# Scores of the mLSTM chunks as four 64x64 products, without their masked quarter

## The chip, the cores and the metric

The kernel runs on one core of a Trainium2 chip. The metric is the device time of one execution in microseconds (us). A comparison uses the median of several executions; the profile is one execution taken by the hardware profiler.

## The reference

The program joins two blocks. The first is an mLSTM cell over batch 4, 8 heads, 768 tokens and head size 40; the second is a feed-forward block on the 3072 tokens with 320 features, 2048 hidden units and exact GELU.

```python
for t in range(S):
    m_new = np.maximum(f_gate[:, :, t] + m, i_gate[:, :, t])
    f_stab = np.exp(f_gate[:, :, t] + m - m_new)
    i_stab = np.exp(i_gate[:, :, t] - m_new)
    m = m_new
    C = f_stab[..., None, None] * C + i_stab[..., None, None] * np.einsum('bhd,bhe->bhde', vt, kt)
    n = f_stab[..., None] * n + i_stab[..., None] * kt
    h_tilde = np.einsum('bhde,bhe->bhd', C, qt)
    denom = np.maximum(np.abs(np.einsum('bhd,bhd->bh', n, qt)[..., None]), 1.0)
    y[:, :, t] = sigmoid(o_gate[:, :, t]) * h_tilde / denom
x = y.transpose(0, 2, 1, 3).reshape(B * S, H * D)
h = x @ w_in
out = (0.5 * h * (1.0 + erf(h / sqrt(2)))) @ w_out
```

## The kernel before, in words

The 768 tokens are cut into 6 chunks of 128 (index `c`, 0 to 5). A cell is one chunk of one batch, `n = 4 * c + b`. Inside a chunk the recurrence is written as attention: `scores` computes k·q for the 128 source tokens s (partitions) and the 128 target tokens t (columns) of each of the 8 heads. The result is multiplied by decay weights W, and `values` multiplies the product with v. What came before the chunk enters through a carried state (`carry`, and `carry_two` for two batches at once from chunk 2 on). Weights are zero where s > t, so a quarter of each head's 128x128 scores (s in the second half, t in the first) is computed and then multiplied by zero.

Heads go in pairs. In the transposed tiles kT and qT one head of a pair lies on partitions 0 to 63 and the other on 64 to 127 (`halves`, index `hip`); the 40 features of a head are padded to 64. For each pair `scores` (L469) issues two products of 64 rows, 128 stationary and 128 moving columns (L479), one in each half of the array's rows, into two PSUM banks. VectorE then multiplies each bank by the weights with one 128x512 instruction (L482).

The other operations that the prediction follows, by line:

- `load` (L129, issue at L135): q, k, v and o-gate of a cell into SBUF, one transfer each, issued by SP. From chunk 2 on q and k for the scores come by `load_blocks` (L138, issues at L145) and are transposed by VectorE (`turn_half`, L430). The token-major k and v are still loaded for the state and the values; three buffers take turns. `load_M` (L154, L162 and L165) brings the running maximum, from which W is made.
- `mask` (L378, L381): GpSimd's affine_select writes 1e30 where s > t. `weights` (L384, L407): ScalarE turns the tile into exp(-M + a), head by head, with the per-token bias aT on partitions.
- `weigh_values` (L464, L466): v times ewT, again a factor for each partition. It feeds the products of v and k that update the state (L538 in `carry_two`); L531 there is the product of q with the old state. VectorE takes L531's result (L547) and updates the state (L554 on GpSimd, L555 on VectorE).
- `values` (L564): L573 on TensorE, L581 on VectorE. `finish` (L583, L586 to L591), `twice` (L597), `turn_y` (L599, L608 and L618) and `split_x` (L623) normalise y and turn it into the input of the feed-forward block.
- `up` (L747, L768 and L779 on TensorE, L783 on ScalarE) and `down_steps` (L831, L844 on TensorE; L857, L861, L867, L874 on the others) are the feed-forward block of a chunk. L682 are sums of the second weight matrix, made once while chunk 1's products run; L672 and L700 to L702 are sums needed by its products.
- `gates_turned` (L215, L222): the gate tables aT, ewT and gT are transposed by TensorE and copied by VectorE, once at the start.

The order is written out by hand: `FRONT` for the first two chunks and the conversion of the 64-bit weights, and `DOWN` for each later chunk, in which the letters of chunk c + 1's cell steps stand between the products F of chunk c's feed-forward block. In `DOWN` M is mask, W weights, S scores, C carry_two, V values, K and Q the transposes of k and q, D weigh_last, Y finish, X turn_y, R split_x, L and B the loads for the last batch, Z and N sums on VectorE:

```python
M0 Z M1 W0 F L3 F B3 W1 Z Z F S0 Z S1 K2 C0 M2 Z G0 G1 G2 G3 V0 Z V1 W2 Z F Q2 K3 Q3 Y0 M3 D3 F F W3 F Z S2 S3
C2 V2 V3 F N F Y1 X0 R0 Y2 F F Y3 X1 R1 F X2 R2 F X3 R3 F
```

So the attention of a chunk has two rounds: S0 S1 C0 V0 V1, and S2 S3 C2 V2 V3. Each engine keeps to the order of its own instructions.

Of the kernel before, what the change touches and what calls it, by code (L numbers as in the profile page):

```python
# [14 lines left out]
OP = mybir.AluOpType  # L15

P = 128
# [22 lines left out]
def kernel(  # L40
# [16 lines left out]
    nc = tc.nc  # L57

    B, H, S, D = q.shape
    L = P  # L60
    NCH = S // L
    NP = H // 2
# [7 lines left out]
    R = P // 2  # L70
# [30 lines left out]
    aT = const.tile([P, NCH, BH], F32, name="aT")  # L101
    ewT = const.tile([P, NCH - 1, BH], F32, name="ewT")
    gT = const.tile([P, NCH - 1, BH], F32, name="gT")
# [22 lines left out]
    def out_of(n):  # L126
        return ob[n % NLD].rearrange("p (h d) -> p h d", d=D)

    def load(n, first=0, end=4):  # L129

        if n >= NCH * B:
            return
        c, b = divmod(n, B)
        for src, dst in ((q, qb), (k, kb), (v, vb), (o_gate, None))[first:end]:
            nc.sync.dma_start(out=dst[turn_of(n)][:, :, 0:D] if dst else out_of(n),  # L135
                              in_=src[b, :, c * L:(c + 1) * L, :].rearrange("h p d -> p h d"))

# [12 lines left out]
    def turn_of(n):  # L150

        return n % NLD if n < 2 * B else (n - 2 * B) % NQ
# [19 lines left out]
    for t in vb:  # L172
# [4 lines left out]
                            pattern=[[0, P]], channel_multiplier=1)  # L177
    nc.gpsimd.memset(beyond, 0.0)
    nc.gpsimd.affine_select(out=beyond, in_=beyond, compare_op=OP.is_ge, fill=1.0e30, base=0, pattern=[[1, L]],
                            channel_multiplier=-1)  # L180
# [7 lines left out]
    a = gates.tile([BH, NCH, L], F32, name="a")  # L188
    M = gates.tile([BH, NCH, L], F32, name="M")
    ew = gates.tile([BH, NCH - 1, L], F32, name="ew")  # L190
    gg = gates.tile([BH, NCH - 1, L], F32, name="gg")
# [4 lines left out]
    for j in range(3):  # L196
        m = slice(BH * j, BH * (j + 1))
# [16 lines left out]

    def gates_turned(*parts):  # L215

        for src, dst in parts:
            n = dst.shape[1]
            pg = ps_tr.tile([P, n, BH], F32, name="pg", tag="tr")
            for c in range(n):  # L220
                nc.tensor.transpose(pg[:, c, :], src[:, c, :], ident[0:BH, 0:BH])
            nc.vector.tensor_copy(out=dst, in_=pg)  # L222

    def gates_of(c0, c1):

        flat = lambda t: t[:, c0:c1].rearrange("p c l -> p (c l)")
        nc.vector.tensor_tensor_scan(out=flat(bl), data0=flat(keep), data1=flat(f_sb), initial=0.0,
                                     op0=OP.mult, op1=OP.add)
        nc.vector.tensor_tensor(out=a[:, c0:c1], in0=i_sb[:, c0:c1], in1=bl[:, c0:c1], op=OP.subtract)
        for c in range(c0, c1):  # L230
            nc.vector.tensor_tensor_scan(out=M[:, c], data0=a[:, c], data1=a[:, c], initial=m0[:, c:c + 1],
                                         op0=OP.max, op1=OP.max)
            if c + 1 < NCH:
                nc.vector.tensor_tensor(out=m0[:, c + 1:c + 2], in0=bl[:, c, L - 1:L], in1=M[:, c, L - 1:L],
                                        op=OP.add)

    def decays_of(e0, e1, g0, g1):

        e, g = slice(e0, e1), slice(g0, g1)
        nc.vector.tensor_tensor(out=ew[:, e], in0=a[:, e], in1=M[:, e, L - 1:L].to_broadcast([BH, e1 - e0, L]),  # L240
                                op=OP.subtract)
        nc.vector.tensor_tensor(out=gg[:, g], in0=m0[:, g0 + 1:g1 + 1].unsqueeze(2).to_broadcast([BH, g1 - g0, L]),
                                in1=M[:, g0 + 1:g1 + 1], op=OP.subtract)
        nc.scalar.activation(out=ew[:, e], in_=ew[:, e], func=AF.Exp)
        nc.scalar.activation(out=gg[:, g], in_=gg[:, g], func=AF.Exp)

    def decays_turned(e0, e1, g0, g1):
        e, g = slice(e0, e1), slice(g0, g1)
        gates_turned((ew[:, e], ewT[:, e]), (gg[:, g], gT[:, g]))

    def decays_last(g0, g1):
        g = slice(g0, g1)
        pd = ps_tr.tile([P, g1 - g0, BH], F32, name="pd", tag="tr")
        nc.tensor.matmul(pd.rearrange("p c n -> p (c n)"), last, gT[:, g].rearrange("p c n -> p (c n)"),
                         start=True, stop=True)
        nc.vector.tensor_copy(out=dec[:, g], in_=pd)
# [4 lines left out]
    for j in range(3):  # L261
        part = M_parts[BH * j:BH * (j + 1)]
        nc.vector.tensor_copy(out=part, in_=left)
        if j < 2:
            nc.vector.tensor_tensor(out=M_left[:, j], in0=left, in1=part, op=OP.subtract)
            left = M_left[:, j]
    gates_turned((a[:, 0:1], aT[:, 0:1]))
    warm(6)

    def second_gates():  # L270
        gates_of(1, 2)
        nc.sync.dma_start(out=M_d[0], in_=M[:, 1])
        gates_turned((a[:, 1:2], aT[:, 1:2]))
        decays_of(0, 2, 0, 1)

    def later_gates():
        gates_of(2, NCH)
        nc.sync.dma_start(out=M_d[1:].rearrange("c p l -> p c l"), in_=M[:, 2:])
        gates_turned((a[:, 2:], aT[:, 2:]))
        decays_of(2, NCH - 1, 1, NCH - 1)  # L280


# [1 line left out]
    for name, w in (("in", moe_w_in), ("out", moe_w_out)):  # L284
        rows, cols = w.shape
# [66 lines left out]
    halves = (slice(0, R), slice(R, P))  # L352
# [7 lines left out]
    def unread(bank):  # L360
        for _ in range(idle[0]):
            nc.tensor.matmul(bank, ident, ident, start=True, stop=True, skip_group_check=True)
        idle[0] = 0
# [4 lines left out]
    class Cell:  # L368
# [9 lines left out]
        def mask(self, b):  # L378

            t = Mb[self.c * B + b]  # L380
            nc.gpsimd.affine_select(out=t, in_=t, compare_op=OP.is_ge, fill=1.0e30, base=0,  # L381
                                    pattern=[[0, H], [1, L]], channel_multiplier=-1)

        def weights(self, b):  # L384

# [83 lines left out]
        def scores(self, b):  # L469
            n = self.c * B + b  # L470
            kT, qT = self.kT.pop(b), self.qT[b]

            pool, tag = (ps_tr, "tr") if self.c > 0 and b % 2 else (ps_mm, "a")
            ps = [pool.tile([P, NP, L], F32, name="ps", tag=tag) for hip in range(2)]
            unread(ps[0][:, 0, :])
            for p in range(NP):
                for hip in range(2):
                    r = halves[hip]
                    nc.tensor.matmul(ps[hip][:, p, :], kT[r, p, :], qT[r, p, :], start=True, stop=True)  # L479
            for hip in range(2):  # L480
                w = W[n].rearrange("p (m two) t -> p m two t", two=2)[:, :, hip, :]
                nc.vector.tensor_tensor(out=w, in0=ps[hip], in1=w, op=OP.mult)  # L482

        def carry(self, b):

# [72 lines left out]
        def read(self, b):  # L558

            self.reads.append(b)  # L560
            if self.c > 1 and self.reads.count(b) == 2:
                load(self.c * B + b + NQ, 1, 3)
# [36 lines left out]
        def turn_y(self, b):  # L599
            n, t = self.c * B + b, slice(b * L, (b + 1) * L)  # L600
            if self.c > 0:
                px = ps_tr.tile([P, NX + 1, L], F32, name="px", tag="tr")
            else:
                px = ps_mm.tile([P, NX + 1, L], F32, name="px", tag="b")
            unread(px[:, 0, :])
            for k in range(NX + 1):
                y = ob[n % NLD][:, k * P:(k + 1) * P] if k < NX else y_rest.rearrange("p two r -> p (two r)")
                nc.tensor.transpose(px[:, k, :], y, ident)  # L608
            self.turned.append(b)
            if len(self.finished) > len(self.turned):  # L610
                self.twice(b + 1)
            if self.c == 0:
                nc.scalar.copy(out=first_x[:, :, t], in_=px)
                return
            self.px[b] = px
            if "x" not in parts:
                parts["x"] = raw.tile([P, NX + 1, TG], F32R, name="x_hi", tag="x", bufs=1)
            nc.scalar.activation(out=parts["x"][:, :, t], in_=px, func=AF.Copy, scale=PART)  # L618
            if self.c == 1 and b < NQ:
                load(n + NLD, 1, 3)  # L620
            load(n + NLD, 3, 4)
# [18 lines left out]
    w_sums, parts, fars, w_hi, w_lo, w_mid = [], {}, [], [], [], {}  # L640
# [268 lines left out]
    def cell_steps(c, letters, before=None):  # L909
# [7 lines left out]
    first_g = Hidden(False)  # L917
    n_pieces = range(len(pieces))
    steps = dict(P=fetch, L=lambda n: load(n, 0, 2), O=lambda n: load(n, 2, 4), B=load_M, E=second_gates, N=later_gates,
                 I=keep_clock, k=warm, D=lambda: decays_turned(0, 2, 0, 1), Q=lambda: decays_turned(2, NCH - 1, 1, NCH - 1),  # L920
                 d=lambda: decays_last(0, 1), q=lambda: decays_last(1, NCH - 1),
                 A=in_turn(first_up_steps(0)), U=in_turn(first_up_steps(1)), F=in_turn(first_down_steps(first_g)),
# [4 lines left out]
    for c in range(1, NCH):  # L927
        g, later, steps = Hidden(True), [], {}
# [5 lines left out]
        products, late = down_steps(c, g)  # L934
# [32 lines left out]
```

## Time and profile before

| | us |
|---|---|
| median of 3 runs | 484.65 (484.27 to 485.49) |
| the profiled execution's own time | 484.47 |
| its span, first to last instruction | 482.7 |
| TensorE busy, of the span | 473.8 |
| VectorE | 346.4 |
| ScalarE | 222.3 |
| GpSimd | 69.5 |
| L479, the scores' products: records, mean of one | 384, 279 ns |
| L482, the multiplication by weights: instructions, mean of one | 48, 682 to 685 ns |
| L381, masks: instructions, mean of one | 20, 1.09 to 1.14 us |

In the lines of the profile, PE is TensorE's products, PEld its weight loads, DVE VectorE, ACT ScalarE, POOL GpSimd, and SPq the queue of SP, which issues transfers. L and a number is a line of the kernel. A float32 product appears as two records. Products overlap in the array, so the duration of one record is longer than the distance to the next; the distance is what counts in a row of them. The granted TensorE clock is 1.000 over the whole span.

### The profile page before, as it was taken

The numbers are of one execution on the slowest core, as the hardware profiler recorded it, in microseconds if no ns is written. First come the engines' busy times: TensorE is split into PE (matmuls) and PEld (weight loads), VectorE is DVE, ScalarE is ACT, GpSimd is POOL, SyncE is SP. The second block draws the span as 40 slices with busy tenths as digits, with TensorE's granted clock in tenths as the row PEclk, the third lists the DMA queues.
The fourth block names the chain that finished last, engine by engine and source line by source line (L and its number), as shares of the span: only waits on it lengthen the run. The fifth ranks groups of instructions, "written<-read, shape, count | busy, mean of one in ns | idle before, by whom it ended". The sixth has DMA issues, their size and how long they took to land.

```text
span 482.7 us, 11369 instructions
## 1 busy us (share of the span) xinstructions
PE 473.8 (98%) x4484; PEld 413.6 (86%) x4484; DVE 346.4 (72%) x744; ACT 222.3 (46%) x477; POOL 69.5 (14%) x108
## 2 busy tenths in 40 slices
PE   7999999999999999999999999999999999999997
PEld 7788888877777999977999977999977899977997
DVE  7899699898979997747498757498857397724321
ACT  6977999844632941112951113961103852112300
POOL 3001200001000234200144200145000212000000
PEclk9999999999999999999999999999999999999999
DMA  9998955379320365921264922265921250100001
GB/s 174 202 220 180 208 145 140 90 184 218 104 27 7 36 126 76 206 50 22 31 117 72 216 50 25 29 127 75 205 49 22 32 90 3 47 9 0 1 1 54
DMA packets 168021, 44.28 MB, mean 92 GB/s; under 512 B 154176, under 2 KB 161504, under 8 KB 167968
## 3 DMA queue, kind: packets, MB, share of 16 engines
q1 hardware_dynamic: 167968, 43.56, 46.4%
q8 instruction: 35, 0.57, 0.5%
q14 instruction: 18, 0.15, 0.1%
HBM read 39.52 MB, written 4.01 MB: 90 GB/s over the span
## 4 chain that ended last, share of the span: by engine, by line
PE 91%; DVE 4%; SPq 1%; ACT 1%; DMA 1%; issue 1%; DVEq 0%
PE po L844 32%; PE pu L768 21%; PE po L821 7%; PE pu L713 6%; PE pu L779 6%; PE ph L573 5%; PE ps L479 5%; PE pf L531 2%; PE pu L719 2%; PE px L608 2%; PE pf L538 1%; SPq L135 1%; PE pt L453 1%; ACT g L783 1%; PE pf L498 1%; DMA ob<-in_o_gate_dram 1%
## 5 line engine op out<-in xcount | busy, mean ns | idle before, releaser
L844 PE MATMUL po<-w_out,g 128*128 128x160 f32 x640 | 91.2, 300 | 0.0
L844 PEld LDWEIGHTS po<-w_out,g 128*128 128x128 f32 x640 | 87.8, 190 | 1.8 <-ACT g L783 1.8
L783 ACT ACTIVATE g<-pu 128x512 f32<-128x512 f32 x80 | 40.8, 616 | 53.5 <-PE pu L779 53.3
L844 PE MATMUL po<-w_sums,sums 128*128 128x160 f32 x320 | 47.2, 302 | 0.0
L844 PEld LDWEIGHTS po<-w_sums,sums 128*128 128x128 f32 x320 | 44.2, 190 | 0.4
L618 ACT ACTIVATE x_hi<-px 128x384 fp32r<-128x384 f32 x20 | 9.8, 489 | 70.6 <-PE px L608 70.6
L768 PE MATMUL pu<-x_hi,w_in_hi 128*128 128x512 f32 x160 | 41.7, 402 | 0.0
L700 DVE TENSOR_TENSOR sums<-g 128x512 f32<-128x512 f32 x20 | 13.8, 689 | 38.6 <-ACT g L783 38.6
L768 PE MATMUL pu<-x_lo,w_in_lo 128*128 128x512 f32 x160 | 40.7, 396 | 0.0
L407 ACT ACTIVATE W<-W,aT 128x128 f32<-128x128 f32 x128 | 39.1, 389 | 0.4 <-POOL W L381 0.2
L482 DVE TENSOR_TENSOR W<-ps,W 128x512 f32<-128x512 f32 x40 | 25.5, 685 | 15.9 <-ACT W L407 10.9
L768 PEld LDWEIGHTS pu<-x_hi,w_in_hi 128*128 128x128 f32 x160 | 28.5, 188 | 9.4 <-ACT g L783 4.1
L768 PEld LDWEIGHTS pu<-x_lo,w_in_lo 128*128 128x128 f32 x160 | 30.1, 188 | 7.2
L821 PE MATMUL po<-w_out,g 128*128 128x320 f32 x128 | 35.3, 434 | 0.0
L857 DVE TENSOR_TENSOR o_sb<-po,o_sb 128x320 f32<-128x320 f32 (+1 forms) x27 | 12.6, 465 | 28.9 <-PE po L844 24.8
L821 PEld LDWEIGHTS po<-w_out,g 128*128 128x128 f32 x128 | 24.0, 190 | 9.8 <-DVE w_out L348 0.2
L768 PE MATMUL pu<-x_all,w_in_mid 128*128 128x512 f32 x80 | 31.7, 396 | 0.1
L783 ACT ACT_TABLE_LOAD x5 | 6.4, 1283 | 55.1 <-DMA blocks<-in_k_dram 27.5
L768 PE MATMUL pu<-x_all,w_mid 128*128 128x512 f32 x80 | 31.7, 396 | 0.0
L419 POOL MEMSET g<- 32x1024 f32 x8 | 7.6, 944 | 155.8 <-ACT W L407 155.6
L713 PE MATMUL pu<-first_x,w_in 128*128 128x256 f32 x128 | 28.9, 382 | 0.0
L381 POOL TENSOR_SCALAR_AFFINE_SELECT W<-W 128x1024 f32<-128x1024 f32 x16 | 18.1, 1137 | 67.3 <-DMA W<-M_d 58.9
(180 smaller groups left out, 907.8 us busy)
## 6 DMA issues: line engine op xcount, KB each, us to landing
W<-M_d SPq DMA_DIRECT2D x16, 512.0 KB, 5.7
bits<-in_moe_w_in_dram SPq DMA_DIRECT2D x20, 256.0 KB, 4.1
bits<-in_moe_w_out_dram SPq DMA_DIRECT2D x16, 320.0 KB, 3.6
ob<-in_o_gate_dram SPq DMA_DIRECT2D x24, 160.0 KB, 3.9
out_dram<-o_sb SPq DMA_DIRECT2D x24, 160.0 KB, 1.9
vb<-in_v_dram SPq DMA_DIRECT2D x22, 160.0 KB, 5.1
kb<-in_k_dram SPq DMA_DIRECT2D x22, 160.0 KB, 4.8
g<-M_d SPq DMA_DIRECT2D x4, 512.0 KB, 4.2
```

What stands on the lines that cost most here:

```text
L381: nc.gpsimd.affine_select(out=t, in_=t, compare_op=OP.is_ge, fill=1.0e30, base=0, pattern=[[0, H], [1, L]], channel_multiplier=-1)
L407: nc.scalar.activation(out=W[n][:, h, :], in_=src, func=AF.Exp, scale=-1.0, bias=aT[:, self.c, r:r + 1])
L479: nc.tensor.matmul(ps[hip][:, p, :], kT[r, p, :], qT[r, p, :], start=True, stop=True)
L482: nc.vector.tensor_tensor(out=w, in0=ps[hip], in1=w, op=OP.mult)
L573: nc.tensor.matmul(ph[r, h, :], Pm[:, h, r], vb[turn_of(n)][:, h, :], start=True, stop=True)
L700: nc.vector.tensor_tensor(out=s1, in0=a21, in1=a22, op=OP.add)
L713: nc.tensor.matmul(banks[-1][e][:, i - i0, :], in_tile(i, x)[:, e, i % 2 * P:(i % 2 + 1) * P], first_x[:, x, t0:t1], start=(x == 0 and i = ...
L768: nc.tensor.matmul(pus[i][e], w[k][:, e, i * P:(i + 1) * P], x[:, k, :], start=(n == 0 and k == 0), stop=False, skip_group_check=True)
L779: nc.tensor.matmul(pu[e], w[r, i // 2, i % 2 * P:(i % 2 + 1) * P], x[r, NX, :], start=False, stop=(n == 2), skip_group_check=True)
L783: nc.scalar.activation(out=g.t[:, HF * e + i, :], in_=pu[e], func=AF.Gelu, scale=4097.0)
L821: nc.tensor.matmul(po[b], g.t[:, f, b * L:(b + 1) * L], w_out[:, f, :], start=(f == 0), stop=(f == NF - 1))
L844: nc.tensor.matmul(bank[at][:, i, :], lhs(j, t), rhs(j), start=(first and i == 0 and j == 0), stop=(i == n - 1 and j == HF - 1), skip_grou ...
```

## The change

For chunks 2 to 5 a head's scores are computed in products of 64 source tokens: the first 64 source tokens against all 128 targets, the second 64 against the last 64 targets only. The masked quarter is never computed. Four of these stand side by side in the array: two by rows (the heads of a pair), and two by columns (a pair of heads 0 to 3, and a pair of heads 4 to 7). For that, heads 4 to 7 keep the two halves of the source tokens swapped on the partitions: the first 64 tokens lie on partitions 64 to 127. What has source tokens on partitions follows: token-major k and v are loaded in three transfers instead of one, the mask has three parts, and the gate tables aT and ewT get two more copies each for these heads. The multiplication by weights covers only what was computed, in three regions for each bank. Values and state sum over all source tokens, so they stay as they are.

```diff
         for src, dst in ((q, qb), (k, kb), (v, vb), (o_gate, None))[first:end]:
+            if dst and n >= 2 * B:
+                x, to = src[b, :, c * L:(c + 1) * L, :].rearrange("h p d -> p h d"), dst[turn_of(n)][:, :, 0:D]
+                h0, h1 = slice(0, H // 2), slice(H // 2, H)
+                nc.sync.dma_start(out=to[:, h0], in_=x[:, h0])
+                for i in range(2):
+                    nc.sync.dma_start(out=to[halves[i], h1], in_=x[halves[1 - i], h1])
+                continue
...
             nc.vector.tensor_copy(out=dst, in_=pg)
+            if rotated:
+                there, here = [t.rearrange("p c (b h) -> p c b h", h=H)[:, :, :, H // 2:] for t in (dst, pg)]
+                for i in range(2):
+                    nc.vector.tensor_copy(out=there[R * i:R * i + R], in_=here[R * (1 - i):R * (1 - i) + R])
...
-            nc.gpsimd.affine_select(out=t, in_=t, compare_op=OP.is_ge, fill=1.0e30, base=0,
-                                    pattern=[[0, H], [1, L]], channel_multiplier=-1)
+            if self.c < 2:
+                parts = ((t, 0),)
+            else:
+                parts = ((t[:, 0:H // 2], 0), (t[0:R, H // 2:], -R), (t[R:P, H // 2:, 0:R], 0))
+            for x, base in parts:
+                nc.gpsimd.affine_select(out=x, in_=x, compare_op=OP.is_ge, fill=1.0e30, base=base,
+                                        pattern=[[0, x.shape[1]], [1, x.shape[2]]], channel_multiplier=-1)
...
-            for p in range(NP):
-                for hip in range(2):
-                    r = halves[hip]
-                    nc.tensor.matmul(ps[hip][:, p, :], kT[r, p, :], qT[r, p, :], start=True, stop=True)
+            if self.c < 2:
+                products = [(slice(0, P), p, slice(0, P), slice(0, P)) for p in range(NP)]
+            else:
+                products = [(halves[x ^ y], y * NP // 2 + p, halves[x], slice(R * x, P))
+                            for p in range(NP // 2) for x in range(2) for y in range(2)]
+            for rows, p, s_half, t in products:
+                for r, bank in zip(halves, ps):
+                    nc.tensor.matmul(bank[rows, p, t], kT[r, p, s_half], qT[r, p, t], start=True, stop=True)
+            every, m = slice(0, P), NP // 2
+            regions = (((every, slice(0, NP), every),) if self.c < 2 else
+                       ((every, slice(0, NP), halves[1]), (halves[0], slice(0, m), halves[0]), (halves[1], slice(m, NP), halves[0])))
             for hip in range(2):
                 w = W[n].rearrange("p (m two) t -> p m two t", two=2)[:, :, hip, :]
-                nc.vector.tensor_tensor(out=w, in0=ps[hip], in1=w, op=OP.mult)
+                for x in regions:
+                    nc.vector.tensor_tensor(out=w[x], in0=ps[hip][x], in1=w[x], op=OP.mult)
```

## The prediction

> **What bounds the kernel now.** I read the busy shares first, then the chain of waits in order of time, then the stretches of one stage, then the order of VectorE's instructions. The page says that TensorE is nearly always occupied:
>
> ```profile
> PE 473.8 (98%) x4484; PEld 413.6 (86%) x4484; DVE 346.4 (72%) x744; ACT 222.3 (46%) x477; POOL 69.5 (14%) x108
> ```
>
> The chain of waits (start, length, what) shows what that means from 157 us on: one TensorE block follows the other with hardly a gap. This is the attention part of chunk 3 (counting from 0), and that of the last chunk:
>
> ```profile
> 238.66 1.99 PE ps L479 x32
> 240.64 1.07 PE pf L531 x64
> 241.71 1.06 PE pf L538 x32
> 242.78 1.87 PE ph L573 x64
> 244.64 8.89 PE po L844 x64
> ...
> 384.50 1.99 PE ps L479 x32
> 386.49 1.07 PE pf L531 x64
> 387.56 2.00 PE ph L573 x64
> ```
>
> The scores of two batches (L479), then carry (L531, L538), then values (L573). Values need the scores multiplied by the decay weights on VectorE (L482). So VectorE has the carry's 2.1 us as cover in most chunks, and 1.1 us in the last chunk, which has no L538. Each chunk does this twice (batches 0 and 1, then 2 and 3).
>
> How loaded is VectorE there? In the stretch between the two rounds (length, then PE, PEld, DVE, ACT, POOL busy) it works 8.35 of 8.90 us:
>
> ```profile
> 244.60:253.50 8.90, 8.90 (x68) 8.73 (x66) 8.35 (x18) 3.73 (x13) 2.66 (x4) 1.00 0.74 149
> ```
>
> The chunk with 311 us shows its order in the timeline (start, length from first start to last end):
>
> ```profile
> 312.77 2.48 DVE L482 TENSOR_TENSOR W<-ps,W 128x512 f32<-128x512 f32 x4 [2.84 <-ACT W L407]
> 315.17 1.41 DVE L430 STREAM_TRANSPOSE kT<-blocks 64x512 f32<-64x512 f32 x2
> 316.62 0.57 DVE L547 TENSOR_TENSOR far<-pf,gT 128x164 f32<-128x164 f32 x2
> 317.10 0.65 DVE L555 TENSOR_TENSOR state<-state,pf 64x164 f32<-64x164 f32 x2
> ```
>
> The transposes follow the multiplications without a gap, so what makes L482 longer makes everything up to the next round later. The 2.84 before L482 is idle time; the label names ScalarE, but L482 starts 1.29 us after the scores start, when they end.
>
> **What the Trainium skill says.** "TensorEngine Tiling (Array Packing)", Tiling Modes: tiles of 64x64 work independently, four at once, and changing the mode drains the array. The trace agrees: L531, already 64x64, needs 1.07/16 = 67 ns for four records; and inside a score block the pairs follow every 112 ns, so 16 pairs make 1.79 of the 1.99 us, the other 0.20 being the block's two edges. "TensorE: Matmul & The Clock Gate", LDWEIGHTS: a load costs columns/1.2, 53 ns for 64 columns whatever the rows; L573, with 41 moving columns, needs 1.87/32 = 58 ns for two, so loads bound it. "VectorE: DVE Perf Modes", Two Vector instructions with no wait between them: an instruction that starts in another group of partitions than the one before waits until that has ended. The trace agrees: two L547 of 320 ns on all partitions take 0.57 together, two L555 of 317 ns on the lower and then the upper half 0.65. A handoff on the same quadrant is thus 0.083 us early, one across halves 0.013 late.
>
> **The change, part by part.**
>
> *TensorE.* Per cell, 8 products of 64 rows x 128 columns (16 records, in twos) become 16 of 64x64 (32 records, in fours): two fours of 128 moving columns and two of 64, two records each. One record of 128 columns paces at 112 ns (above); 64 columns take half, and not less than the weight load: 58 ns. A cell: 4 x (112 + 58) = 0.68 us instead of 0.90. Two cells: 1.36 + 0.10 for entry = 1.46, as the next block (L531) has the same tile shape and no edge. Saved: 1.985 - 1.46 = **0.525 us per round**, 8 rounds (4 chunks x 2): 4.2 us if nothing else moved. That fours keep their pace at 128 columns is not shown: L538 moves different data through two column tiles at 58 ns for two records of 34 ns streaming each, less than one after the other. Bound the other way: serial column tiles, 212 + 112, make a round 0.7 us longer than now.
>
> *VectorE.* Each 128x512 multiplication (682 ns) becomes three: 128x256, lower 64x128, upper 64x128. From 512 and 164 elements, time is elements/0.96 + 0.15 us: 0.416, 0.283, 0.283 (the skill's VectorE page, TRN2 errata, prices the same operation at (N+151)/0.96, an estimate within 10 ns). One bank: 0.416 - 0.083 + 0.283 + 0.013 + 0.283 = 0.912, where it was about 0.60. A round: 4 x 0.912 + 3 x 0.013 = 3.69 instead of 2.48, **+1.20 us**. It starts 0.18 earlier, so it ends 1.02 later.
>
> *First round.* Times from its start. VectorE: starts 1.11; the second batch's fifth piece ends at 1.11 + 1.85 + 1.54 = 4.50, so its second head may go at 4.57. TensorE: 1.46 + 1.05 (L531) + 0.95 (L538) + 0.94 (first values) + 0.12 (first head) = 4.52. Stall 0.05: the round gains 0.5 in the chunks at 238 and 311. At 164 two weight sums (0.47 us, L682) lie between the batches' multiplications: stall 0.52, gain 0. At 384 there is no L538: stalls 0.09 + 0.91, **loss 0.44**.
>
> *Second round.* VectorE comes to it late by 1.02, less the idle bits on the way (0.10 before L857, 0.55 in the last chunk), while TensorE comes earlier. What helps is GpSimd: its mask and VectorE's two-input and copy operations block each other:
>
> ```profile
> 251.53 1.09 POOL L381 TENSOR_SCALAR_AFFINE_SELECT g<-g 128x1024 f32<-128x1024 f32 x1 [4.04 <-DMA g<-M_d]
> 251.99 0.66 DVE L588 TENSOR_SCALAR den<-far 128x8 f32<-128x8 f32 x1
> 253.72 0.71 DVE L597 COPY y_rest<-ob 128x128 f32<-128x128 f32 x1
> 254.72 1.29 DVE L482 TENSOR_TENSOR W<-ps,W 128x512 f32<-128x512 f32 x2 [0.30 <-PE ps L479]
> ```
>
> L588 takes 0.17 and L597 0.23 elsewhere, so 0.5 each was lost here. Later arrival dodges part of that. Carried through, I get stalls of 0.6 (at 179), 0.9 (253), 0.6 (326) and 1.0 (398): the round nets about +0.1, +0.4, +0.1, +0.4.
>
> *Chunk by chunk*: at 164: 0 and +0.1, less half of the 0.9 us that TensorE stood in the values at 184.8 ("issue", no releaser; a VectorE stall in the same place would overlap it): -0.4. At 238: -0.1. At 311: -0.4, but L597 ends there at 344.14, when the transposes of y (L608) already stand, so a later VectorE takes it back: 0. At 384: +0.9. Sum **+0.4**.
>
> *GpSimd.* 16 masks of 1.09 us become 0.63 + 0.63 + 0.41 (elements as 128x128, 0.29, to 128x1024, 1.09): +0.6 each. ScalarE's exponentials wait for them, but may start after the first piece. I cost it at nothing; cover: L482 comes to the last batch later than before.
>
> *SP and DMA.* 32 loads of k and v become 96: 64 more issues, 0.45 each, 7 us per chunk, ahead of weights for later cells, o-gate loads and stores. Bytes and packets stay. SP has room:
>
> ```profile
> SPq L145 <- DVE kT L430: 57.1, 8, 10.7
> ```
>
> that is, it stood 57 us waiting for VectorE to free the block buffer. v of batch 3, issued at 248.6, would land some 1.5 us later; GpSimd's weighing (253.6) would end about 255.8, and L538 reads it at about 256. If that cover goes: up to 0.5 per chunk, but in front of a values stall that would swallow it.
>
> *Front.* Four copies of 64 partitions (about 0.18 each) follow the two L222 copies of the gate tables at 13.0 and 18.1. VectorE idles 0.58 at 16.7 and 0.59 at 19.3, which takes most; the second pair delays gT, its product and the chain to 27 us: **+0.2**.
>
> Sum: +0.4 + 0.2 = +0.6 on the profiled execution's own 484.47 (span 482.7 and 1.8 around it): 485.1. The median of the runs, 484.65, lies 0.2 above it, inside their scatter. Differences under 0.3% (1.45 us) are about what a measurement here can't tell from no change.
>
> **Rivals.**
>
> *The upper-half pieces are not held* (17%): handoffs as for L547. A round on VectorE is then 4 x (0.416 + 0.283 + 0.283 - 0.25) = 2.93; stalls fall by about 0.6 to 0.75, and the four chunks give -1.7, -1.1, -0.8, -0.3: with the front 480.8; half of it 482.7. For it: nothing but that the skill calls the rule a model. Against: the 0.65 of L555.
>
> *The twelve pieces hand over more dearly* (40%), slower: each has its own waits on TensorE, ScalarE and GpSimd. An operation behind an extra wait instruction follows after 0.105 instead of 0.034 here (L591), so +0.05 a piece is possible. Eleven pieces lie ahead of the last values, 7 of 8 rounds have no slack left: 11 x 0.05 x 7 = 3.9 us, 488.5. It decides from 0.012 a piece (0.9 us more). Serial column tiles (212 ns) would end here too: TensorE +0.7 a round, 5.6 us, partly in place of stalls. Against: waits that are met overlap the operation before (L482's do now).
>
> *It doesn't run in fours*: the order alternates row halves within and column halves between products, like L531's, which does. Counted in the slower case.
>
> **How the numbers follow.** No measurable change, 43%: 485.1, own range 483.3 to 486.1. Faster 17%, slower 40%. The range of 8 in 10 takes half of the not-held case and nearly all of the dear one: 482.3 to 488.3.
>
> **What would show it.** Right: L479 falls from 1.99 to about 1.46 per round on the chain; six L482 groups per batch at 416 and 283 ns; VectorE's round 3.7 us; values (L573) interrupted by L482, most in the last chunk; up to 4 us fewer in L479 and as much more in L573. Wrong: L482 rounds under 3.1 or over 4.2 us, fours slower than 130 ns, or L538 waiting for GpSimd's weighing.

## The result, and the profile after

The changed kernel takes 490.46 us (median of seven runs, 487.27 to 493.58) against 485.37 for the kernel before, run beside it (484.27 to 486.49): ratio 1.0104, 95% interval 1.0068 to 1.0141. It is slower by 5.1 us; 485.1 was predicted, with 488.3 as the upper end. The profiled execution took 490.46 us, with a span of 488.7.

Some lines have moved: the scores' products are L499 now (L479 before), their multiplication L506 (L482), the carry L555 and L562 (L531, L538), the values L597 (L573), the turning of gate tables L228 (L221), the down products L868 (L844). L233 is the new copy that swaps halves.

The page's first two parts, busy time of the engines and TensorE's clock in 40 slices, hold the surprise at once. TensorE is as busy as before, but its clock is 6 tenths in the second slice, 12 to 24 us after the start, where nothing of the scores of the later chunks runs yet:

```profile
PE 475.7 (97%) x4740; PEld 414.5 (85%) x4740; DVE 358.8 (73%) x812; ACT 222.8 (46%) x477; POOL 85.2 (17%) x140
...
PEclk9699999999999999999999999999999999999999
```

I cut both traces at the same products and compared the pieces. A chunk goes from its first up product to that of the next; the predicted column has the parts of the prediction's sum:

| stretch, us | before | changed | difference | predicted |
|---|---|---|---|---|
| start to first down product | 92.96 | 98.05 | +5.09 | +0.2 |
| from there to the first up product | 35.56 | 35.41 | -0.15 | 0 |
| chunk with the rounds at 164 and 179 | 74.56 | 73.86 | -0.70 | -0.4 |
| at 238 and 253 | 72.90 | 73.05 | +0.15 | -0.1 |
| at 311 and 326 | 72.95 | 73.37 | +0.42 | 0 |
| at 384 and 398 | 71.03 | 72.19 | +1.16 | +0.9 |
| from there to TensorE's last product | 59.18 | 59.18 | 0.00 | 0 |

In this execution the attention part loses 1.03 us where 0.4 was predicted; the front loses 5.09 where 0.2 was.

**The front.** The stretches 12 to 24 and 24 to 36 us (length, then PE, PEld, DVE, ACT and POOL busy, granted clock, DMA share, GB/s), first of the kernel before, then of the changed one:

```profile
12.00:24.00 12.00, 11.05 (x141) 8.94 (x142) 10.45 (x27) 11.68 (x40) 0.00 (x0) 1.00 0.98 201
```

```profile
12.00:24.00 12.00, 10.57 (x70) 8.72 (x69) 8.31 (x24) 8.68 (x28) 0.00 (x0) 0.64 1.08 198
24.00:36.00 12.00, 12.00 (x177) 10.40 (x176) 10.70 (x26) 10.39 (x24) 0.00 (x0) 0.93 0.77 161
```

TensorE gets 70 products done where it did 141, at a mean clock of 0.64. The clock's record says that it was halved from 15.41 to 25.65 us, 10.24 us on end. The timeline shows what comes just ahead of that:

```profile
13.30 0.46 DVE L233 COPY aT<-pg 64x64 f32<-64x64 f32 x2
...
14.35 0.52 ACT L255 ACTIVATE ew<-ew 32x384 f32<-32x384 f32 x1 [0.75 <-DVE ew L251]
...
14.93 0.37 PE L228 MATMUL pg<-ident,ew 32*128 32x32 f32 x3 [0.67 <-ACT ew L255]
```

The two small copies stand on VectorE in front of the subtraction that makes `ew` (L251). It and the exponential (L255) come 0.6 us later, and TensorE, which turns `ew` next, waits 0.67 us (in brackets). In the kernel before, the same products stand 0.6 us earlier and have no wait:

```profile
14.33 0.37 PE L221 MATMUL pg<-ident,ew 32*128 32x32 f32 x3
```

After the wait the half clock begins. Whether the one makes the other takes more than this execution to tell; the experiments with the copies alone and with the wait filled are about that.

**The scores.** The chain of waits at the chunk that had its rounds at 238 and 253:

```profile
242.87 1.50 PE ps L499 x64
244.37 0.92 PE pf L555 x64
245.28 1.06 PE pf L562 x32
246.34 1.05 PE ph L597 x36
247.40 0.12 issue
247.51 1.02 PE ph L597 x28
...
261.59 0.90 issue
```

The scores take 1.50 us instead of 1.99, so the fours do stand side by side. The carry's first part takes 0.92 instead of 1.07: with the same tile shape ahead of it, it loses its edge too. Values in turn are broken up, in the first round by 0.12 us and in the second by 0.90. The last of these has no releaser: the profile shows nothing that TensorE waited for. The experiments below say what it is. VectorE's round in this chunk:

```profile
243.86 3.83 DVE L506 TENSOR_TENSOR W<-ps,W 128x256 f32<-128x256 f32 x12 [2.61 <-ACT W L423]
```

3.83 us, where 3.69 was predicted and 2.48 stood before. In the first of the chunks the chain leaves TensorE altogether, for SP's split loads (L138, L140) and this one of them:

```profile
182.49 3.75 DMA vb<-in_v_dram
```

v of batch 3 lands at 186.24, GpSimd weighs it only then, and the chain goes on from GpSimd to VectorE's last six pieces. This is no cost, though. VectorE's twelve pieces run from 186.21 to 190.02 with no gap longer than 0.03 us, and right before them VectorE works from 180.4 on with none longer than 0.11. So VectorE itself is late here; the load has used up the cover that the prediction named, and no more. The chunk as a whole still gains.

### The profile page after: what moved, and what is told of

Read it like the earlier page. It is cut to its first block, busy times and chain, and to the rows that moved or that the text cites. A ratio compares the mean times of both kernels' runs of the same rounds, so it can differ in the third digit from the quotient of the medians.

```text
span 488.7 us, 12190 instructions
## 1 busy us (share of the span) xinstructions
PE 475.7 (97%) x4740; PEld 414.5 (85%) x4740; DVE 358.8 (73%) x812; ACT 222.8 (46%) x477; POOL 85.2 (17%) x140
## 4 chain that ended last, share of the span: by engine, by line
PE 80%; DVE 9%; ACT 3%; SPq 3%; issue 2%; DMA 2%; POOL 1%; DVEq 0%; POOLq 0%; ACTq 0%
PE po L868 26%; PE pu L792 21%; PE po L845 7%; PE pu L803 6%; PE pu L737 5%; PE ps L499 3%; PE ph L597 3%; SPq L152 2%; PE pu L743 1%; PE px L632 1%; PE pt L469 1%; ACT g L807 1%; DVE g L506 1%; DMA vb<-in_v_dram 1%; PE pf L555 1%
## 5 line engine op out<-in xcount | busy, mean ns | idle before, releaser
L868 PE MATMUL po<-w_out,g 128*128 128x160 f32 x640 | 91.2, 300 | 0.0
L868 PEld LDWEIGHTS po<-w_out,g 128*128 128x128 f32 x640 | 87.8, 190 | 1.8 <-ACT g L807 1.8
L868 PE MATMUL po<-w_sums,sums 128*128 128x160 f32 x320 | 47.2, 302 | 0.0
L868 PEld LDWEIGHTS po<-w_sums,sums 128*128 128x128 f32 x320 | 44.2, 190 | 0.4
L506 DVE TENSOR_TENSOR W<-ps,W 64x128 f32<-64x128 f32 (+2 forms) x88 | 32.1, 395 | 15.8 <-ACT W L423 8.4
L397 POOL TENSOR_SCALAR_AFFINE_SELECT W<-W 128x512 f32<-128x512 f32 (+3 forms) x40 | 27.5, 704 | 70.7 <-DMA W<-M_d 63.7
```

The lines of the kernel that those rows point to most:

```text
L397: nc.gpsimd.affine_select(out=x, in_=x, compare_op=OP.is_ge, fill=1.0e30, base=base, pattern=[[0, x.shape[1]], [1, x.shape[2]]], channel_m ...
L506: nc.vector.tensor_tensor(out=w[x], in0=ps[hip][x], in1=w[x], op=OP.mult)
L868: nc.tensor.matmul(bank[at][:, i, :], lhs(j, t), rhs(j), start=(first and i == 0 and j == 0), stop=(i == n - 1 and j == HF - 1), skip_grou ...
```

## The experiments

My theory after these readings: the front loses through TensorE's clock, not through the copies' own 0.5 us; in the attention part what TensorE gains turns into waits for VectorE's pieces. The rivals: the copies' own work makes the front late; the loads and masks cost; the fours gain less than they seem. Each kernel ran beside the kernel before on the same chip, whose median is given. The edits are shown in short form, in part in words. "At full clock" means runs with a mean TensorE clock of 0.9985 or more, since in nearly every kernel here the runs below it are the slower ones.

### The copies alone, in the kernel before

```
 gates_turned(...): nc.vector.tensor_copy(out=dst, in_=pg)
+    if rotated: two copies of 64 partitions, from pg into a tile that nobody reads
```

> The kernel before with only the four extra 64-partition copies of the gate tables at their place in the front; they write a spare tile that nothing reads, all else is as before. Front theory (the copies hold back ew, its exponential and its transposes, TensorE idles about 0.7 us more near 14 us, and its clock is halved for some 10 us): 486.5 to 490.5, that is 1 to 5 us over the kernel before, part of the runs with a mean clock of about 0.99, and chunks 2 to 5 as long as before. Chunk theory (the loss comes from VectorE's six pieces and SP's extra transfers in chunks 2 to 5): within 0.4 us of the kernel before.

486.99 us (twenty runs) against 484.70, ratio 1.0037 (1.0019 to 1.0055). The profiled execution, with its clock at 1.00 all through the front, has its first down product at 93.57, 0.6 later than before. TensorE waits for `ew` there as in the changed kernel:

```profile
PE pg L221 <- ACT ew L249: 0.7, 1, 0.7
```

(who waited <- for whom: us, times, longest). So this wait doesn't lower the clock in every execution. But of the twenty runs sixteen had a mean clock below 0.9985, of the 26 runs of the kernel before only four; the four at full clock have a median of 484.96, against 484.60 for the kernel before at full clock. So the copies' own work costs 0.4 to 0.6 us, and with the same copies the clock drops in most runs and makes 2.3 of it, by the medians.

### The copies moved behind the decay tables

```
     (in the changed kernel)
-    if rotated: copy at once
+    turns_left.append((dst, pg))       # copied by rotate(), at the end of later_gates() and behind decays_last(1, NCH - 1)
```

> The changed kernel with the four extra copies moved: those of aT behind the two subtractions of ew and gg, those of ewT behind the product of gT and its copy. Front theory: the clock stays at 1.000, the front is as long as before to within 0.5 us, and what remains of the change is what its chunks 2 to 5 lost in the trace, about 1.0 us: 485.7 to 487.0. Chunk theory: no better than the changed kernel, 489 to 491.

486.75 us against 484.70, ratio 1.0043 (1.0026 to 1.0060). `ew` is no longer late, three of seven runs fall below 0.9985 instead of six of seven, and the first down product comes at 95.69. The expected full clock didn't come: the profiled run has one half-clock stretch, 15.2 to 18.6 us, without any wait for `ew`. So that wait isn't the only way to a lower clock either. At full clock the median is 486.39 (four runs), 1.8 above the kernel before at full clock.

### The wait filled, the copies left in place

```
     (in the changed kernel)
-    ... K L2 Q s0 ...
+    ... K L2 k4 Q s0 ...               # k4: four products of constants, ahead of the turning of ew
```

> The changed kernel with one edit: four products of constants that nobody reads stand on TensorE ahead of the first turning of the decay tables, where it stood idle for 0.67 us. If what the change loses in the front is TensorE's halved clock after that idle time, the products cost nothing (they take 0.7 us of the 0.67 us that was idle anyway), the clock stays at 1.00 in the front, the first down product starts at 93.5 to 94.5 us instead of 98.05, and the median falls from 490.5 to 486 to 487. If the loss is the copies' own work on VectorE and what it makes late, the front stays where it is: first down product after 96 us, median above 489.

487.14 us (17 runs) against 484.63, ratio 1.0055 (1.0040 to 1.0070). TensorE works where it waited, and the stretch reads:

```profile
12.00:24.00 12.00, 11.29 (x143) 9.55 (x142) 10.89 (x30) 11.13 (x38) 0.00 (x0) 1.00 1.00 202
```

The clock is 1.00 and the first down product comes at 93.60, 4.45 us earlier than in the changed kernel, with every copy in its old place and four products more. Four of 17 runs fall below 0.9985, where six of seven did with the wait left open. This decides for the clock as what makes the front late. It also speaks for the wait as what makes the clock's fall frequent, though these two kernels didn't run side by side. The 13 runs at full clock have a median of 486.72, 2.1 above the kernel before at full clock. The median misses the expected 487 by a little. The profiled run itself took 489.69, for it stood 2.28 us in the second values of one chunk, without a releaser, and then had 3.41 us of half clock: see "Where the gaps without a releaser come from".

### The pieces alone, in the kernel before

```
-    nc.vector.tensor_tensor(out=w, in0=ps[hip], in1=w, op=OP.mult)
+    for x in regions:                  # the three regions of the change
+        nc.vector.tensor_tensor(out=w[x], in0=ps[hip][x], in1=w[x], op=OP.mult)
```

> The kernel before with its own score products, loads, masks and front; only VectorE's multiplication is cut into the three pieces of the change, which leaves a quarter of each W (the masked one: exponentials, not products) unmultiplied. Each round on VectorE should last 3.7 to 3.9 us instead of 2.48. If pieces reach the end of a round, values are held by 0.9 us in the last chunk's first round and by 0.1 to 0.6 in each second round: together 1.5 to 3 us, median 486 to 487.7. If the old products, which leave values later, hide the pieces, nothing moves: 484.5 to 485.

488.42 us against 484.63, ratio 1.0073 (1.0055 to 1.0091): +3.8 us, more than the 3 that I expected at most. The four chunks give +0.09, +0.74, +1.33 and +1.59. The waits of TensorE show that values are only part of it:

```profile
PE ph L577 <- DVE W L486: 1.4, 3, 0.6
...
PE px L612 <- DVE y_rest L601: 1.0, 1, 1.0
```

The chunk with +1.33 has no wait in its values at all. VectorE carries its lateness through two rounds to the end of the cell, and the products that turn y (px, L612) wait 0.97 us for it. Slower VectorE work is paid where VectorE is late next, not where it was lengthened.

### Loads and masks alone, in the kernel before

```
-    one transfer for k, one for v; one mask
+    three transfers each (heads 0 to 3; heads 4 to 7 in two token halves, not swapped); three masks of the change's sizes
```

> The kernel before with only the traffic of the change: k's and v's loads from chunk two on as three transfers each and the masks of these chunks in three instructions, no halves swapped (the result is that of the kernel before). If SP and GpSimd hide this, as the prediction costed it, the median stays within 0.5 of the kernel before: 484.2 to 485.2. If late loads reach the carry's products or late masks reach ScalarE's exponentials, up to 0.5 us in each of four chunks: 485.7 to 487.

485.02 us (22 runs) against 484.63, ratio 1.0010 (0.9999 to 1.0020). At full clock 484.60 against 484.59. SP and GpSimd hide this traffic, as the prediction costed it. The late v load in the changed kernel's chain comes with the combination, and the trace shows nothing there that it delayed.

### All 128 targets, one multiplication

```
     (the copies moved as above)
-    slice(R * x, P)                    # second 64 source tokens: targets 64 to 127
+    slice(0, P)                        # all targets
-    for x in regions: ...
+    nc.vector.tensor_tensor(out=w, in0=ps[hip], in1=w, op=OP.mult)
```

> As the kernel with late copies, but the second 64 source tokens are multiplied against all 128 targets, so nothing is skipped, and VectorE multiplies each bank with one 128x512 instruction as before. The four-wide products, the three-part masks and the three-part loads stay. If VectorE's pieces make the stalls in the values: a round of scores 1.9 us (16 fours of 112 ns and one edge), no stalls behind the multiplication, chunks 2 to 5 shorter than before by about 0.1 us a round, 484.3 to 485.5. If the loads or masks make them: 1 us over the kernel before, as with late copies.

482.49 us against 484.70, ratio 0.9950 (0.9934 to 0.9966): faster than expected, and than the kernel before. The scores take 1.91 us a round, and the carry's first part 0.91: 0.08 and 0.16 less, 1.9 us in eight rounds, two thirds of it from the edge between tile shapes. All six runs had the full clock; the kernel with late copies, which has the same front, had it in four of seven.

### Natural fours: no swap at all

```
     for p in range(NP):
-        for hip in range(2): matmul(ps[hip][:, p, :], kT[r, p, :], qT[r, p, :])
+        for s in halves if self.c > 1 else (slice(0, P),):
+            for r, bank in zip(halves, ps): matmul(bank[s, p, :], kT[r, p, s], qT[r, p, :])
```

> The kernel before with its own loads, masks, front and multiplication; only each product of 64 rows x 128 columns is cut into two of 64x64 columns, all against 128 targets, so that four stand side by side with no swap of halves. TensorE should save 0.08 us in the scores and 0.15 in the carry's first product of each of 8 rounds, 1.8 us in all, with nothing added elsewhere: median 482.0 to 483.2. If fours need the swap to run side by side, the scores take about 3.5 us a round instead of 1.99 and the median is above 494.

482.88 us (nine runs) against 484.63, ratio 0.9962 (0.9944 to 0.9980), as expected. The chain, at the chunk of 238:

```profile
238.17 1.91 PE ps L479 x64
240.08 0.91 PE pf L531 x64
240.99 1.06 PE pf L538 x32
```

So 64x64 products with 128 targets run in fours without any swap, copy, split load or piece. What the swap adds is that the four products side by side are equally long when the masked quarter is left out; a version that leaves it out without the swap wasn't run. This version and the last one beat both kernels; their intervals overlap.

### Natural fours in all chunks

```
-        for s in halves if self.c > 1 else (slice(0, P),):
+        for s in halves:
```

> The kernel before with natural fours in all chunks, not only from chunk two on. If TensorE's path also sets the pace in the first two chunks' scores, 0.23 us less in some of their eight cells, and the 512 instructions more shift the later gaps by nothing: median 482.0 to 483.0 against 482.9 with fours from chunk two on. If VectorE and ScalarE set the pace there, no difference; if the chopped products of the front make TensorE want for instructions there, 483.5 to 484.5.

483.97 us against 485.04, ratio 0.9979 (0.9964 to 0.9994). It beats the kernel before, but is above the 482.0 to 483.0 expected if TensorE set the pace in the first two chunks, and I see no gain over fours from chunk two on. The two ran on different chips, so the difference between them stays open.

### The masked quarter filled with zeros, one multiplication

This keeps the short products and takes the pieces away: small bf16 products of zeros write the quarter, so that it may be multiplied too.

```
     (the copies moved as above)
+    matmul(bank[halves[1 - y], two pairs, 0:R], zeros, zeros)     # four times a cell
-    for x in regions: ...
+    nc.vector.tensor_tensor(out=w, in0=ps[hip], in1=w, op=OP.mult)
```

> As the kernel with late copies, but the masked quarter of each bank is filled with zeros by four bfloat16 products of 64x64 with 128 columns per cell (about 60 ns together), and VectorE multiplies each bank with one 128x512 instruction. TensorE keeps the saving of 0.5 us a round less 0.12 for the fill, VectorE's round is 2.5 us as before. If the pieces are what took the saving: 8 rounds of 0.35 to 0.4, 481.8 to 483.0. If the multiplication's latency or the loads bind all the same: 484.5 or more.

489.23 us against 484.70, ratio 1.0085 (1.0054 to 1.0116): a clear miss. Values wait 0.2 us for VectorE instead of 2.2 (1.2 and 1.0 in the changed kernel), so the pieces are indeed gone. In their place:

```profile
PE ph L609 <- issue: 4.9, 4, 2.1
```

and on the chain, in the chunk of 253:

```profile
256.54 0.05 PE ph L609
256.59 2.05 issue
258.64 2.54 PE ph L609 x63
```

TensorE stands 2.05 us with nothing to wait for that the profile shows, and another 2.04 us in the next chunk. With both the clock is halved: for 3.41 us from 260.0, 1.4 us after the first gap, and for 6.83 us from 335.1, still within the second.

### Where the gaps without a releaser come from

The trace holds the packets of each engine's instruction queue. Queue 8 moves packets of 16 KB, of the kernel before and of the changed one:

```profile
q8 instruction: 35, 0.57, 0.5%
```

```profile
q8 instruction: 37, 0.61, 0.6%
```

(packets, MB, share). The kernel before has 4484 products and as many weight loads, 8968 instructions, and 35 x 256 is 8960; the changed one has 9480, and 37 x 256 is 9472. So a packet holds 256 TensorE instructions. I numbered TensorE's records in the traces, its few semaphore instructions included, and looked up every gap. The 2.05 us end at number 5312, the 2.04 at 7104, the 0.90 of the changed kernel at 5312, the 0.90 of the kernel before (at 184.8 us) at 3520: all are 192 modulo 256, give or take one. And each ends shortly after a packet of queue 8 has landed: 1.42, 1.46, 1.31 and 1.48 us. The Trainium skill ("Runtime: NRT & Kernel Launch", Instruction fetch mechanics) says that each engine has its instructions in a small memory, refilled by its own DMA queue in blocks of 16 KB, 256 instructions, and that crossing a block is mostly hidden. The block agrees. Hidden it isn't here: in the rounds, 256 instructions (nearly half of them weight loads) run in as little as 2.3 us.

Three kernels test this by moving the blocks against the code:

```
     gates_turned((a[:, 0:1], aT[:, 0:1]))
-    warm(6)
+    warm(2)
+    for _ in range(72): one product of constants, 32x32, bf16     # 128 TensorE instructions more in all
```

In the zero-filled kernel:

> The kernel with the zero-filled quarter, with 128 more TensorE instructions (72 products of constants of 32x32 that nobody reads, in place of four large ones of the same kind) near the start, where TensorE waits in any case. If TensorE stands for want of its next 256 instructions, all gaps without a releaser end again at an instruction number of 192 modulo 256, 1.25 to 1.55 us after a 16-KB packet of its instruction queue has landed; as that is now 128 instructions earlier in the code, the two gaps of 2.05 us in the second values shrink below 0.7 or go, the values' issue waits fall from 4.9 us to under 1.5, and the median from 489.2 to 483 to 486. If the gaps come from the zero-filling products or the banks, they stay in the second values of the same chunks, about 2 us each, and the median stays at 488 to 490.

490.26 us against 485.04, ratio 1.0096 (1.0062 to 1.0131). The gaps of 2 us in the second values of both chunks are gone from there, as the instruction theory says and the rival, the zero-filling products or their banks, denies. But as many have come up elsewhere:

```profile
184.51 0.69 PE ph L613 x22
185.21 2.07 issue
```

2.07 us one chunk earlier, and 1.64 us at 333.27, in the carry ahead of those second values and thus 128 instructions earlier; the five largest end at numbers 3776, 4800, 5568, 6592 and 7104, again 192 modulo 256, 1.32 to 1.54 us after a landing. So the cause held and my numbers didn't: I had reckoned with gaps that vanish, and they moved. The small products also brought 3.41 us of half clock at 7.8 us, which delays the first down product by 0.45 us.

In the changed kernel with the wait filled:

> The changed kernel with TensorE's wait in the front filled by unread products, and the same 128 instructions more near the start. If missing instructions cost the change 0.5 to 2.5 us in the values at chunk three's second round, that gap goes, and the median falls from 487.1 to 485 to 486.3; what stays above the kernel before is the front's 0.6 us and the values waiting for VectorE's pieces. If those waits only hid behind the gap, they come out in its place and the median stays at 486.5 to 487.5.

489.86 us against 485.04, ratio 1.0093 (1.0057 to 1.0130). The gap of 2.28 us is gone; in its place values wait 0.49 us for VectorE, which it had covered. But 1.27 us came up in the chunk before and 2.84 in the chunk after, both again at 192 modulo 256. The expected gain of 1 to 2 us is lost to these and to half clock in the front and after the gap.

In the kernel with natural fours:

> The kernel before with natural fours, and 128 TensorE instructions more near the start. Its three gaps without a releaser (0.26, 0.46 and 0.44 us, at instruction numbers 3008, 3520 and 6848) should go or move to other multiples; all gaps that are left end at 192 modulo 256. Median 481.5 to 483.3, as the new places may be better or worse. If the gaps have another cause they stay where they are.

486.32 us (22 runs) against 485.04, ratio 1.0018 (1.0000 to 1.0037), a miss. Its three gaps left their places for numbers 3776, 4800 and 8128 and grew from 1.2 to 1.9 us in all, and the front lost 2 us to the small products. The one shift that I tried, by 128 instructions, helped none of the three kernels.

Over the fourteen traces, 32 gaps of more than 0.2 us after 160 us end at a number of 192 modulo 256, each 1.23 to 1.62 us after a landing. What sets when a packet is sent for (in the gaps it starts up to 2.7 us after TensorE has passed the block before) wasn't tried.

## Why the prediction was wrong

**Front, +0.2: this step failed.** It measured +5.1 in the profiled execution. The step asked where VectorE idles afterwards, and found 0.58 and 0.59 us to take the copies up. It didn't ask who waits for the instruction queued right behind them. That was `ew`, then its exponential, then TensorE, which has nothing else in order there: 0.67 us. The copies' own cost is 0.4 to 0.6 us (the copies alone); the rest is the clock, 10.24 us at half rate: with that one wait filled, the front came 4.45 us earlier. No rival had a lower clock in it. By the medians, filling that one wait takes the change's loss from 5.1 to 2.5 us, so by leaving the clock out the step was short by about 2.6 us in a usual run, and by more in the profiled one. Why one run loses the clock and another doesn't stays open. The other part of the miss lies in the rounds.

**TensorE, 0.525 us a round: mechanism right, size low.** The scores went to 1.50 us (1.46 worked out), and the carry's first part lost 0.15 that I hadn't counted though I had named its missing edge: 0.64 a round. The bound of serial column tiles is refuted.

**VectorE, 3.69 us a round: 3.83.** The lower piece starts 0.083 us early as said. The upper piece, and the next bank's first, start 0.031 late more often than 0.013. The rival without a hold is refuted.

**Rounds, +0.4: +1.03, and nearer +1.5 by the medians** (an estimate: the filled kernel's 2.1 at full clock, less 0.6 for the copies in the front). By chunks, sign and pattern are right: a gain in the first chunk, the largest loss in the last, which has no L562 as cover, and there a first round of +0.60 where 0.44 was worked out. By rounds there is luck in it. In the first chunk the first round lost 0.59 us where 0 was worked out, and the second gained 1.27, as the gap of 0.90 us that the kernel before had there is gone. The 0.9 us worked out for the values at 253 came out as 0.90, but by another cause, missing instructions; with that gap moved away, VectorE alone holds values by 0.49. Values waited 2.2 us for VectorE in all, and the second and third chunk lost 0.25 and 0.42 more than said, with gaps of 0.90 and 0.43 at block ends. The prediction took the one "issue" gap that it saw as something that VectorE's stall would overlap, and didn't ask what makes it. The kernel before has one such gap of over 0.2 us after 160 us, the changed kernel three; that more TensorE instructions in less time make them likelier is argued, not tested.

**GpSimd, SP and DMA at nothing: right.** At full clock 484.60 against 484.59, and the late load of v in the changed kernel delays nothing that its trace shows.

**How the parts add up.** Pieces alone cost 3.8 us. The shorter fours save TensorE 8 x 0.64 = 5.1, of which full fours alone bring 1.8. If savings and cost added up, the attention part would gain 1.3 us; it loses 1.03. Of the difference of 2.3, 0.76 is gaps at block ends (1.66 us in the changed kernel, 0.90 before). For the rest I argue, without a run that shows it, that values come earlier on TensorE and their operands later on VectorE, so that the two meet in one wait. The dear-handoff rival came nearest in time, 488.5, but by luck and not for its reason: VectorE's round is 0.14 us longer than worked out, not 0.55. Its sum is off besides: 3.9 us on top of the main case's 485.1 is 489.0; 488.5 is 3.9 on top of the median before.

## What to carry to other kernels

Before you slip even a half-microsecond instruction into an engine's queue, follow what is queued behind it up to TensorE: a new wait of well under a microsecond in a sparse stretch can cost many times its length through the clock, in some runs and not in others; here four unread products in that wait took half of the loss away by the medians. Split products for their tile shape alone and keep one multiplication; work left out of one engine was no gain here, as it cut another engine's instruction into pieces. Count TensorE's instructions too, where they are short.

## What the runs showed of the hardware

- **The clock can drop after short waits.** The Trainium skill ("TensorE: Matmul & The Clock Gate", What's actually happening) gives an idle window of about 3.4 us ahead of half rate. All half-clock stretches inside these kernels last 3.41, 6.83 or 10.24 us, which agrees with a window of that length. The waits were shorter than the page says, and the measurement decides: in the rounds each of the six gaps of 1.64 to 2.84 us has a half-clock stretch that starts within 1.5 us of its end, and none of those of 1.30 us or less has. In the front 0.67 us more of waiting in a sparse stretch went ahead of 10.24 us at half clock, with TensorE at work, but 0.65 us in the copies alone did not. In the front of the zero-filled kernel with 72 small products, TensorE was busy for 2.92 of 3.41 us and the clock still fell for the next 3.41. What the clock goes by is open.
- **TensorE can want for instructions.** In no gap did it go on sooner than 1.2 us after the packet with its next 256 instructions had landed, and it stood up to 2.84 us for it. The kernel before already lost 0.90 us so, at 184.8 us.
- **The edge between tile shapes** costs the block that follows, 0.15 us here; it goes when the block ahead has the same shape.
